# A banded-attention and SMeLU kernel on one core: wider bias matmuls, another layout for half of q, and a divided weight load one piece later

## The chip, the cores and the metric

The kernel runs on 1 core of one Trainium2 chip. The metric is the device time in microseconds (us) of one launch, as a median over several runs. Beside the times there is one profiled execution, from which all rows of the profile come.

The engines are called as the profile calls them: PE (matmuls), PEld (weight loads of the same engine), DVE (VectorE), ACT (ScalarE), POOL (GpSimd, which here issues nearly all loads) and SP (SyncE, which issues the stores and the transposing DMAs).

## The reference

```python
# q, k, v: (8, 8, 576, 64) float32; w_in: (512, 2048); w_out: (2048, 512)
scores = q @ k.T / sqrt(64), kept only where |query - key| <= 32, else -1e9
attn   = softmax(scores);  attn_out = attn @ v
x = attn_out.transpose(0, 2, 1, 3).reshape(4608, 512)
h = x @ w_in
g = h if h >= 1, 0 if h <= -1, else (h + 1)**2 / 4
out = g @ w_out                                # (4608, 512) float32
```

The first part is attention in a band of 65 keys around each query, the second a two-layer network over the 4608 rows of its output.

## The kernel before

**Attention.** Heads 0 to 3 live on partitions 0 to 63 and heads 4 to 7 on partitions 64 to 127; this is the index `h`, and `HD[0]`, `HD[1]` are the two partition ranges. q and k are brought to the form "head dimension on partitions" (`qT`, `kT`). For batch 0 PE does this: `tpose` transposes nine slices `j` of 64 (or 2 x 64) columns, and the result is copied out of PSUM by ACT or DVE (line 193). Where the source tile has nine slices of 128 columns, with both halves of heads side by side, `tpose` issues one 128-column transpose for each `j` (line 192); else two of 64 columns (line 190). The first half of batch 0's q (`q32`) is laid out for the former by `cast`, which changes it from float32 to bfloat16 on DVE and ACT. The second half of q and k (`qn[0, 1]`, `kn[0, 1]`, tiles `qh` and `kh`) is loaded by `load_half` as bfloat16 and is transposed in `tposes(0, (0, 1), (1, 1))` at step 1, by line 190.

`scores` computes blocks of 64 keys by 128 queries into two PSUM banks with matmuls of 64x64 tiles (line 230) and takes their exponential on ACT (line 238). Where its argument `eng` is None, the band is made beforehand: `add_mask` (line 209) writes a large negative bias into the same PSUM banks and the score matmuls are added to it. `eng` is None in all of batch 0, and for steps below 14; from then on DVE multiplies the exponentials by a mask (line 204). `add_mask` is called eight times: six times before step 4, and twice for the scores of batch 1 at the steps 12.5 and 13. `sums` multiplies by v and by ones (line 296), and its `end` divides through Ln and Exp on ACT (lines 302, 303) and a multiplication on DVE (line 308 or 311), which writes the rows of `xT`.

**The network.** The main loop counts steps `a`; eight steps make the first layer for 256 rows (`NF` = 8 pieces of 256 columns of w_in; line 490, wide steps line 515). Each step's result goes through ACT (line 534) and DVE (lines 540, 541; in five steps ACT's line 537 and DVE's 538) to `gT`. The second layer is interleaved (lines 450 and 465) and the attention of later batches is spread over the steps by the events `ev`. Step `a` needs w_in's columns 256a to 256a + 255 in the first eight steps. At a = 0 the pieces f = 0 and f = 1 are done together, first with the rows `y = 0` of `xT`, then with `y = 1`.

**The loads.** Every engine works in the order in which its instructions are written. POOL's order at the start is: k's first half, v of batch 0, then the list that `put` runs through:

```python
    cuts = [0, 256, 512, 768, 1024, 1280, 1536, DFF]
    w = [(load_w_in, c0, c1, h) for c0, c1 in zip(cuts, cuts[1:]) for h in range(2)]
    w[3] += ((0, 52, 64),)
    put(w[:4] + [(load_half, 1, t, h) for t in range(2) for h in range(2)] + w[4:])
```

So w_in comes in 14 loads, two for each range of columns, one for each half of the partitions; `w[0]` to `w[3]` are the columns of step 0, `w[4]` and `w[5]` (the third range of columns) those of step 2, and `w[12]` and `w[13]`, which are twice as wide, those of the steps 6 and 7. `w[3]` is issued as two DMAs, of 52 and of 12 partitions. Between `w[3]` and `w[4]` come four loads of the second halves of q and k. The program's loads from POOL go round eight semaphores, and an issue waits for the landing of the load eight places before it. After w_in come w_out's first pieces, and q and k of batch 1.

Of the kernel before, what the change touches and what calls it, by code (L numbers as in the profile page):

```python
# [8 lines left out]
BF = mybir.dt.bfloat16  # L9
# [5 lines left out]
def kernel(  # L15
# [19 lines left out]
    nc = tc.nc  # L35
    B, H, S, D = q.shape
# [11 lines left out]
    const = ctx.enter_context(tc.tile_pool(name="const", bufs=1))  # L48
# [10 lines left out]
    def two_banks(pool):  # L59
        return pool.tile([128, 2, 512], FP, name="bb", tag="bb")  # L60

    ident = const.tile([128, 128], BF, name="ident")
    ones = const.tile([128, 64], BF, name="ones")
    band = const.tile([128, 192], BF, name="band")
    bias = const.tile([128, 192], BF, name="bias")
    mask4 = const.tile([128, 8 * 128], BF, name="mask4")
# [8 lines left out]
    V, P, A = nc.vector, nc.gpsimd, nc.scalar  # L75


    qn, kn, vn = {}, {}, {}
    HD = (slice(0, 64), slice(64, 128))
# [40 lines left out]
    early = ctx.enter_context(tc.tile_pool(name="early", bufs=1))  # L120
# [24 lines left out]
    def put(todo):  # L145
        for fn, *x in todo:
            fn(*x)

    cuts = [0, 256, 512, 768, 1024, 1280, 1536, DFF]
    w = [(load_w_in, c0, c1, h) for c0, c1 in zip(cuts, cuts[1:]) for h in range(2)]  # L150
    w[3] += ((0, 52, 64),)
    put(w[:4] + [(load_half, 1, t, h) for t in range(2) for h in range(2)] + w[4:])
    put([(load_w_out, 0, k, k + 4) for k in (0, 4, 8)] + [(load_rows, 1, t) for t in range(2)] + [(load_w_out, 0, 12, 16)])
    put([(load_v, 1, n) for n in range(4)])
# [10 lines left out]
    def qkT(b, t):  # L165
        if t == 0:
            return qTs[b % 3][:, PAD:]
        if b not in kT:
            kT[b] = ktp.tile([128, NY * S], BF, name="kT")
        return kT[b]  # L170

    def tpose(b, n, t, copy, ps):


        half, part = divmod(n, 2)
        j0, j1 = ((0, 5), (5, 9))[part]
        if b:
            src = qn[b] if t == 0 else kn[b]
            src = [src[:, half + 2 * h] for h in range(2)]
            dst = qkT(b, t).rearrange("d (y e p j) -> d y e p j", y=2, e=2, j=9)[:, half, :, :, j0:j1]  # L180
            like = "d j (e p) -> d e p j"
        else:
            src = (qn, kn)[t][b, half]
            src = src if src.shape[1] == 9 else [src[:, h] for h in range(2)]
            dst = qkT(b, t).rearrange("d (y l p j) -> d l y p j", l=2, p=32, j=9)[:, half, :, :, j0:j1]
            like = "d j (p y) -> d y p j"
        for j in range(j0, j1):
            if isinstance(src, list):
                for h in range(2):
                    nc.tensor.transpose(ps[HD[h], j - j0], src[h][:, D * j:D * j + D], ident)  # L190
            else:
                nc.tensor.transpose(ps[:, j - j0], src[:, j], ident)
        return lambda: copy(dst, ps[:, :j1 - j0].rearrange(like, p=64 if b else 32))
# [10 lines left out]
            eng.tensor_mul(p, p, m)  # L204

    def add_mask(ps, n, w):
        for a in range(2):
            for h in range(2):
                nc.tensor.matmul(ps[h][HD[a], :n * w].rearrange("p (n j) -> p n j", n=n), ident[HD[h], HD[h]],  # L209
                                 bias[HD[h], 64 * h:64 * h + w].rearrange("p (n j) -> p n j", n=1)  # L210
                                 .to_broadcast([64, n, w]),
                                 start=True, stop=False, skip_group_check=True)

    def scores(b, ys, pars, cs, eng, pool=ps_s, w=128, ready=None):

# [98 lines left out]
    def flush():  # L314
        while muls:
            muls.pop(0)()
# [4 lines left out]
    def tp1(pool):  # L321
        if pool is ps_h:
            return pool.tile([128, 8, 128], BF, name="tp", tag="hp")
        return pool.tile([128, 2, 8, 128], BF, name="tp", tag="bb")[:, 0]
# [16 lines left out]
    def cast(x, nm, cut):  # L341

        y = early.tile([128, 9, 2, D], BF, name=nm)
        o, i = y.rearrange("p j h d -> p h j d"), x.rearrange("p h (j d) -> p h j d", d=D)
        V.tensor_copy(o[:, :, :cut], i[:, :, :cut])
        A.copy(o[:, :, cut:], i[:, :, cut:])
        return y.rearrange("p j h d -> p j (h d)")

    with tc.tile_pool(name="ps_p", bufs=1, space=bass.MemoryType.PSUM) as ps_p:
        keep_warm(11, ps_h, "hp")  # L350

        V.memset(qkT(0, 0).rearrange("d (y s) -> d y s", y=NY)[:, :, S // 2:352], 0.0)
        for b in range(LONG):
            V.memset(qkT(b, 0).rearrange("d (y s) -> d y s", y=NY)[:, :, S - PAD:], 0.0)
        V.memset(qkT(0, 1).rearrange("d (y s) -> d y s", y=NY)[:, :, S // 2:320], 0.0)
        qn[0, 0] = cast(q32, "qb", 5)
        qq = [tpose(0, n, 0, (A.copy, V.tensor_copy)[n], tp1(ps_h)) for n in range(2)]
        for x in qq:
            x()
        kk = [tpose(0, n, 1, (A.copy, V.tensor_copy)[n], tp1((ps_n, ps_p)[n])) for n in range(2)]  # L360
        keep_warm(1, ps_h, "hp")
        first = two_banks(ps_s)
        add_mask([first[:, h] for h in range(2)], 4, 128)
        for x in kk:
            x()
        scores(0, (0, 1), (0, 2), (0, 2), None, ready=first)
        scores(0, (0, 2), (0, 1), (2, 3), None, ps_n, 32)
        scores(0, (1, 2), (0, 2), (0, 2), None, ps_p)
        keep_warm(4, ps_h, "hp")
        e0 = sums(0, 0, 0, TB)  # L370
        e1 = sums(0, 1, 0, TB, ps_p)
        keep_warm(5, ps_h, "hp")
        e0()
        e1()
# [44 lines left out]
    for b in range(LONG + 1, B):  # L419
        a = sl[5 * (b - 1) - 7] - 17  # L420
# [75 lines left out]
    for a in range(NF * NB + 2 * NF):  # L496
        wide = WIDE[0] <= a < WIDE[1]
        eng = None if a < 14 else V
        post = [] if a >= 40 else [x for n, x in pairs if n == a] + [a - NF] * (a >= 2 * NF + 2)
        for b, x in loads.get(a, []):  # L500
            if x < 2:
                load_nat(b, x)
            else:
                for n in range(4):
                    load_v(b, n)
        if a == 0 or a > 3:
            flush()
        if a < NF * NB:
            if wide:
                n, f = divmod(a - WIDE[0], 2 * NF)  # L510
                t = WIDE[0] // NF + 2 * n
                r0 = TB * t % RING
                hp = ps_h.tile([128, 2, TB], FP, name="hp", tag="hp")
                for n, kk in enumerate((0, 2, 1, 3)):
                    nc.tensor.matmul(hp.rearrange("p n t -> p (n t)"), w_in[:, kk, 128 * f:128 * f + 128],  # L515
                                     xT[:, kk, r0:r0 + 2 * TB], start=n == 0, stop=n == 3)
                g = gT[:, f, home(t):home(t + 1) + 1:home(t + 1) - home(t)]
            else:
                t, f = divmod(a, NF)
                r0 = TB * t % RING  # L520
                if a in (0,):
                    hps = [ps_h.tile([128, 2, TB], FP, name="hp", tag="hp") for _ in range(2)]
                    for y in range(2):
                        for n in range(2):
                            project(hps[n], f + n, r0, [(j, y + 2 * m) for j in range(2) for m in range(2)], y == 0, y == 1)
                elif not hps:
                    pool, tag = (ps_o, "op") if a == 6 else (ps_h, "hp")
                    hps = [pool.tile([128, 2, TB], FP, name="hp", tag=tag)]
                    project(hps[0], f, r0, [(j, kk) for j in range(2) for kk in (0, 2, 1, 3)], True, True)
                hp = hps.pop(0)  # L530
                g = gT[:, 2 * f:2 * f + 2, home(t)]

            rr = ewp.tile([128, 2, TB], FP, name="rr")
            A.activation(rr, hp, AF.Relu, scale=0.5, bias=0.5)  # L534
            mx = ewp.tile([128, 2, TB], FP, name="mx")
            if a in two_on_act:
                A.activation(mx, rr, AF.Square)
                V.scalar_tensor_tensor(g, hp, 1.0, mx, op0=ALU.max, op1=ALU.min)
            else:
                V.tensor_max(mx, hp, rr)  # L540
                V.scalar_tensor_tensor(g, rr, 1.0, mx, op0=ALU.min, op1=ALU.mult)  # L541
        flush()
        run(a)
        for x in post:
            if x < 16:
                pair(x)
            else:
                for j in range(4):
                    unit(4 * x + j)
        if a >= 40:  # L550
            n = 3 if a < 72 else 4
            for x in range(done, done + n):
                unit(x)
            done += n
        run(a + 0.5)
        for x in xps.get(a, []):
            xpose(*x)
# [30 lines left out]
```

## Time and profile before

| | |
|---|---|
| median of 8 runs | 307.54 us (306.85 to 308.46) |
| the profiled execution's own time | 307.93 us |
| its span | 306.2 us |
| PE busy | 292.6 us (96%) |
| DVE, ACT, POOL busy | 241.4, 190.6, 77.6 us |
| granted PE clock | 1.00 in the five windows read, 0 to 306.2 us |

The span is the time from the first to the last instruction in the profile; 1.73 us of the profiled execution lie around it, and the execution itself lies 0.39 us above the median. Places in the span are given in us from its start.

PE's busy time in five windows of the span is 10.11 of 12.00 us (0 to 12), 11.17 of 14.30 us (12 to 26.3), 15.70 of 15.70 us (26.3 to 42), 242.98 of 248.00 us (42 to 290) and 12.68 of 16.20 us (290 to 306.2).

### The profile page before, as it was taken

Reading aid. Unit: us, or ns where it says so; the run is one execution under the profiler, and the core shown is the slowest. Engines: PE = TensorE matmul, PEld = TensorE weight load, DVE = VectorE, ACT = ScalarE, POOL = GpSimd, SP = SyncE. Lnnn points to the kernel's source line nnn. Section 1 sums busy time; section 2 is a strip of 40 time slices with the busy share of each in tenths; the row PEclk is TensorE's granted clock in tenths of the full one; section 3 lists DMA queues with packets and bytes.
Section 4 is the critical chain, followed back from the end, with each engine's and each line's share of the span. In section 5 each row is a group of like instructions: output and inputs, shape, how many; then the busy total and the mean of one; then the engine's idle time right before and its main releaser. Section 6 shows DMA issues by size and latency. Waiting matters only on the chain.

```text
span 306.2 us, 7809 instructions
## 1 busy us (share of the span) xinstructions
PE 292.6 (96%) x3286; PEld 174.8 (57%) x3324; DVE 241.4 (79%) x378; ACT 190.6 (62%) x318; POOL 77.6 (25%) x93
## 2 busy tenths in 40 slices
PE   8788999999999999999999999999999999999995
PEld 3467878877666766544445444444445444446644
DVE  4278868888888999999988888888888888788700
ACT  3687786738856778667766766665667654444311
POOL 8795771019008206403700730000000000000000
PEclk9999999999999999999999999999999999999999
DMA  9999999999999999995999997551011010010121
GB/s 149 182 177 200 187 182 172 173 166 139 136 202 90 172 149 148 161 157 108 166 125 166 116 171 77 113 112 36 34 36 37 34 36 35 34 36 34 58 82 69
DMA packets 137251, 35.67 MB, mean 117 GB/s; under 512 B 122240, under 2 KB 132992, under 8 KB 137216
## 3 DMA queue, kind: packets, MB, share of 16 engines
q0 software_dynamic: 103056, 18.06, 80.0%
q1 hardware_dynamic: 34016, 16.81, 26.4%
q8 instruction: 26, 0.43, 0.6%
q10 hardware_dynamic: 144, 0.29, 0.4%
q14 instruction: 9, 0.07, 0.1%
HBM read 36.70 MB, written 9.44 MB: 151 GB/s over the span
## 4 chain that ended last, share of the span: by engine, by line
PE 89%; DMA 4%; POOL 3%; issue 2%; ACT 0%; POOLq 0%; ACTq 0%
PE op L450 34%; PE hp L515 23%; PE hp L490 17%; PE bb L296 6%; PE op L465 5%; DMA w_in<-in_moe_w_in_dram 4%; PE bb L230 2%; POOL w_in L112 2%; PE op L441 1%; POOL vn L107 1%; PE tp L190 1%; POOL kh L86 0%; PE bb L209 0%; PE bb L255 0%; POOL step L134 0%
## 5 line engine op out<-in xcount | busy, mean ns | idle before, releaser
L534 ACT ACTIVATE rr<-hp 128x512 f32<-128x512 f32 x144 | 85.6, 595 | 85.6 <-PE hp L515 49.5
L450 PE MATMUL op<-w_out,gT 128*128 128x512 bf16 x460 | 119.5, 379 | 5.0 <-issue 4.8
L540 DVE TENSOR_TENSOR mx<-hp,rr 128x512 f32<-128x512 f32 x139 | 95.7, 689 | 28.1 <-ACT rr L534 26.5
L541 DVE SCALAR_TENSOR_TENSOR gT<-rr,mx 128x512 bf16<-128x512 f32 x139 | 96.4, 694 | 4.8
L515 PE MATMUL hp<-xT,w_in 128*128 128x512 bf16 x320 | 82.1, 379 | 0.0
L450 PEld LDWEIGHTS <-gT 128*128 128x128 bf16 x496 | 46.1, 98 | 47.6
L490 PE MATMUL hp<-xT,w_in 128*128 128x256 bf16 x512 | 66.2, 273 | 2.9 <-DMA w_in<-in_moe_w_in_dram 2.4
L490 PEld LDWEIGHTS <-w_in 128*128 128x128 bf16 x512 | 49.2, 98 | 18.3 <-DMA w_in<-in_moe_w_in_dram 2.0
L515 PEld LDWEIGHTS <-w_in 128*128 128x128 bf16 x320 | 31.3, 98 | 37.8
L99 POOL DMA_DIRECT2D qn<-in_q_dram x12 | 14.6, 1221 | 91.9 <-DMA kT<-kn 89.7
L238 ACT ACTIVATE pt<-bb 128x1024 bf16<-128x1024 f32 (+1 forms) x33 | 32.9, 1002 | 5.0 <-PE bb L230 3.6
L107 POOL DMA_DIRECT2D vn<-in_v_dram x32 | 27.5, 888 | 5.6 <-DMA w_out<-in_moe_w_out_dram 3.1
L308 DVE TENSOR_TENSOR xT<-bb,rc 128x512 bf16<-128x512 f32 (+1 forms) x32 | 21.0, 657 | 9.5 <-ACT rc L303 8.6
L454 ACT COPY osb<-op 128x512 f32<-128x512 f32 x31 | 18.0, 581 | 12.2 <-PE op L450 11.8
L303 ACT ACTIVATE rc<-lr 128x512 f32<-128x512 f32 (+2 forms) x40 | 23.5, 587 | 1.3
L302 ACT ACTIVATE lr<-bb 128x512 f32<-128x512 f32 (+2 forms) x40 | 22.0, 550 | 0.4 <-PE bb L296 0.3
L204 DVE TENSOR_TENSOR pt<-pt,mask 128x1024 bf16<-128x1024 bf16 (+1 forms) x33 | 20.3, 614 | 0.5 <-ACT pt L238 0.5
L296 PE MATMUL bb<-pt,ones 64*64 64x256 bf16 (+3 forms) x352 | 19.4, 255 | 0.1
L296 PE MATMUL bb<-pt,vn 64*64 64x128 bf16 (+3 forms) x712 | 18.3, 204 | 0.1
L296 PEld LDWEIGHTS <-ones 64*64 64x64 bf16 x352 | 10.2, 105 | 12.5 <-issue 12.5
L296 PEld LDWEIGHTS <-vn 64*64 64x64 bf16 x712 | 16.7, 107 | 0.3 <-DMA vn<-in_v_dram 0.3
L465 PE MATMUL op<-w_out,gT 128*128 128x256 bf16 x128 | 16.3, 273 | 0.0
(61 smaller groups left out, 137.8 us busy)
## 6 DMA issues: line engine op xcount, KB each, us to landing
out_dram<-osb SPq DMA_DIRECT2D x35, 256.0 KB, 2.4
vn<-in_v_dram POOLq DMA_DIRECT2D x32, 144.0 KB, 11.1
qn<-in_q_dram POOLq DMA_DIRECT2D x12, 288.0 KB, 7.1
kn<-in_k_dram POOLq DMA_DIRECT2D x12, 288.0 KB, 9.0
w_in<-in_moe_w_in_dram POOLq DMA_DIRECT2D x11, 128.0 KB, 5.0
w_out<-in_moe_w_out_dram POOLq DMA_DIRECT2D x4, 256.0 KB, 8.9
w_out<-in_moe_w_out_dram POOLq DMA_DIRECT2D x2, 512.0 KB, 12.3
kh<-in_k_dram POOLq DMA_DIRECT2D x4, 144.0 KB, 4.9
```

Of the source, the lines that this page charges most:

```text
L107: nc.gpsimd.dma_start(out=vn[b][64 * a:64 * a + 64, :, h], in_=v[b, y:y + 2].rearrange("y s d -> (y s) d") .rearrange("(c r) d -> r c d", ...
L238: A.activation(p, ps[:, :, :w * n].rearrange(like, y=m), AF.Exp, scale=D ** -0.5)
L296: nc.tensor.matmul(bb[HD[h], a, o + c0:o + c1], ones[HD[a]] if c is None else vn[b][HD[a], c, h], p(a, h), start=n == 0, stop=True, skip_g ...
L302: A.activation(lr[:, :, :D0], bb[:, :, D0:2 * D0], AF.Ln)
L303: A.activation(rc[:, :, :D0], lr[:, :, :D0], AF.Exp, scale=-1.0)
L450: nc.tensor.matmul(op[tt], gT[:, j, home(tt // 2), 128 * (tt % 2):128 * (tt % 2) + 128], w_out[:, j], start=j == 0, stop=j == 15)
L465: nc.tensor.matmul(o[:, tt], gT[:, j, p, 128 * tt:128 * tt + 128], w_out[:, j, 256 * half:256 * half + 256], start=not done, stop=len(done ...
L490: nc.tensor.matmul(hp[:, j], w_in[:, kk, 256 * f + 128 * j:256 * f + 128 * j + 128], xT[:, kk, r0:r0 + TB], start=first and n == 0, stop=l ...
L515: nc.tensor.matmul(hp.rearrange("p n t -> p (n t)"), w_in[:, kk, 128 * f:128 * f + 128], xT[:, kk, r0:r0 + 2 * TB], start=n == 0, stop=n == 3)
L534: A.activation(rr, hp, AF.Relu, scale=0.5, bias=0.5)
L540: V.tensor_max(mx, hp, rr)
L541: V.scalar_tensor_tensor(g, rr, 1.0, mx, op0=ALU.min, op1=ALU.mult)
```

## The change

It has three parts. `add_mask` uses a new constant `fold`, two 64x64 identities side by side, so that one matmul with a 64x128 tile writes both partition halves of a bank: two matmuls for each call where there were four. `fold` is written by two DVE additions after `cast`. At step 0 DVE copies the second half of q (`qn[0, 1]`) into a new tile `y`, with both halves of heads side by side for each `j`, so that `tpose` takes line 192's way for it: nine transposes of 128 columns in place of eighteen of 64. And the load that is divided into 52 and 12 partitions is `w[4]` in place of `w[3]`.

```diff
+    fold = const.tile([128, 128], BF, name="fold")
...
-    w[3] += ((0, 52, 64),)
+    w[4] += ((0, 52, 64),)
...
     def add_mask(ps, n, w):
-        for a in range(2):
-            for h in range(2):
-                nc.tensor.matmul(ps[h][HD[a], :n * w].rearrange("p (n j) -> p n j", n=n), ident[HD[h], HD[h]],
-                                 bias[HD[h], 64 * h:64 * h + w].rearrange("p (n j) -> p n j", n=1)
-                                 .to_broadcast([64, n, w]),
-                                 start=True, stop=False, skip_group_check=True)
+        for h in range(2):
+            nc.tensor.matmul(ps[h][:, :n * w].rearrange("p (n j) -> p n j", n=n), fold[HD[h]],
+                             bias[HD[h], 64 * h:64 * h + w].rearrange("p (n j) -> p n j", n=1)
+                             .to_broadcast([64, n, w]),
+                             start=True, stop=False, skip_group_check=True)
...
         qn[0, 0] = cast(q32, "qb", 5)
+        for h in range(2):
+            V.tensor_add(fold[:, HD[h]], ident[:, HD[0]], ident[:, HD[1]])
         qq = [tpose(0, n, 0, (A.copy, V.tensor_copy)[n], tp1(ps_h)) for n in range(2)]
...
         if a == 0 or a > 3:
             flush()
+        if a == 0:
+            y = early.tile([128, 9, 2, D], BF, name="qr")
+            for h in range(2):
+                V.tensor_copy(y[:, :, h], qn[0, 1][:, h].rearrange("p (j d) -> p j d", d=D))
+            qn[0, 1] = y.rearrange("p j h d -> p j (h d)")
         if a < NF * NB:
```

## The prediction

> **What bounds the kernel now.** I read the page's chain first (the chain of work that ended last, shares by engine), then the same chain in order of time for the start, which all three parts of the change touch.
>
> ```profile
> PE 89%; DMA 4%; POOL 3%; issue 2%; ACT 0%; POOLq 0%; ACTq 0%
> ```
>
> ```profile
> 8.17 6.10 DMA w_in<-in_moe_w_in_dram
> 14.27 0.28 issue
> 14.55 4.21 POOL w_in L112 x7
> 18.77 7.48 DMA w_in<-in_moe_w_in_dram
> 26.25 0.05 issue
> 26.29 1.92 PE hp L490 x16
> ```
>
> The columns are start and length in us. Up to 26.25 the chain consists of loads: the issue at 8.17 is the 52-partition part of w[3]; it lands at 14.27, 0.28 later POOL may issue w[6] (eight places on, the same semaphore), seven more issues follow, and the last, w[13], lands at 26.25. From 26.29 on it is PE: in the windows 26.3 to 42 PE is busy for 15.70 of 15.70 us. So the run is a loading stage with its end at w[13], and 279.9 us of PE work in a fixed order behind it. An edit moves the end only if it moves w[13]'s landing or changes PE's time after 26.29.
>
> The waits in the window 26.3 to 45 show what is spare before w[13]:
>
> ```profile
> PE hp L490 <- DMA w_in<-in_moe_w_in_dram: 1.0, 1, 1.0
> ```
>
> PE stood idle for 1.0 us there, with everything earlier done. DVE is busy without a break from 24.12 to 30.3 and then has 1.17 us of idle time, ACT has 1.36 at 30.87. Anything before 26.29 that becomes later by less than 1 us is swallowed.
>
> **Mask matmuls.** Eight calls of four become eight of two. Six are issued before 26.29, under the cover just named (without it each would cost what follows). Two, at 39.43 and 40.97, are on the path. The timeline there:
>
> ```profile
> 39.43 0.11 PEld L209 LDWEIGHTS <-ident 64*64 64x64 bf16 x4 [0.21 <-issue]
> 39.43 0.41 PE L209 MATMUL bb<-bias,ident 64*64 64x512 bf16 x4
> 39.46 0.44 PEld L230 LDWEIGHTS <-kT 64*64 64x64 bf16 x16
> 39.67 0.39 PE L230 MATMUL bb<-qT,kT 64*64 64x128 bf16 x16
> ```
>
> All four mask matmuls begin at 39.43 to 39.44, one on each quarter of the array, and the scores begin 0.24 us later. So the two that are taken away cost nothing today: the path holds one stream of 512 columns, and the two 64x128 matmuls still have it. What is added is a change of tile shape between mask and scores, which now share 64x64. Its price is seen elsewhere, after a 512-column matmul that begins at 7.40:
>
> ```profile
> 7.39 0.10 PEld L339 LDWEIGHTS <-warm 128*128 128x128 bf16 x1
> 7.72 0.11 PEld L209 LDWEIGHTS <-ident 64*64 64x64 bf16 x4 [0.23 <-issue]
> ```
>
> The next shape's weights load 0.32 us after the matmul's start, not right behind its own weights, as line 230's do at 39.46. With the second mask matmul at 39.44 the scores begin at 39.44 + 0.32 = 39.76 instead of 39.67: +0.09 for a call. Lower end: no gap between these two shapes, 0 (not below, since the 512 columns stay). Upper end: the two halves don't run side by side, the second begins at 39.67, the scores at 39.99, +0.32. I take +0.09, since 64-row tiles do run side by side in the row above: two calls, **+0.18**, ends 0 and +0.64.
>
> The rule that speaks against the change is in the Trainium skill, "TensorEngine Tiling (Array Packing)", Tiling Modes, Key Properties: a change of tiling mode, not just of tile, drains TensorE. The 0.21 us before 39.43 agree with it for 128x128 to 64x64. The page gives no time; by it alone the term is a loss of unknown size, and without it the term would be 0.
>
> `fold` costs DVE two additions of 128x64. The nearest row is line 141's 128x128 addition, 0.23 us, so at most 0.46 for both, between 5.87 (end of the cast) and 6.76, where DVE idles 0.89 us for the transposes. Without that cover the first qT copy would be 0.46 later, still inside the 1.0 us.
>
> **Nine transposes.** Line 190's eighteen for q's half and the eighteen for k behind it:
>
> ```profile
> 15.97 0.69 PE L190 MATMUL tp<-ident,qh 128*64 128x128 bf16 x18
> 16.50 0.98 PE L190 MATMUL tp<-ident,kh 128*64 128x128 bf16 x18
> ```
>
> Eighteen take 0.69 us, with 0.22 for a single one, so nine pairs are 0.056 us apart: the two 64-column ones run side by side. Nine of 128 columns (line 192, 0.80 us at 5.92) need as long. Nothing is saved; k's stay as they are and wait for their load (the gap inside the second row). A change of shape now falls between q's and k's transposes, 0.10 us (line 192 to 190 at 6.65), inside that wait.
>
> The copies are new work for DVE, 128x576 bfloat16 each. Bounds: line 204's 0.614 us for 128x1024 gives 0.35, the cast's 0.69 for 128x640 gives 0.62. They wait for qh, which lands at 9.68 + 4.9 = 14.6 and 10.38 + 5.0 = 15.4. Behind them on DVE stands step 0's maximum:
>
> ```profile
> 16.27 0.69 DVE L540 TENSOR_TENSOR mx<-hp,rr 128x512 f32<-128x512 f32 x1 [1.75 <-ACT rr L534]
> ```
>
> The second copy ends at 15.75 to 16.0, before 16.27: hidden in 1.75 us of idle time. PE's transposes, at 15.97 today, wait up to 0.1 for it. Were qh to land 1 us later, line 540 and the transposes would be up to 0.8 late; cover: PE's 1.0. So **0**.
>
> **The divided load.** The number of DMAs stays, and from w[5] on each stands at its old place in the queue and the semaphores. Moved ahead by one place are both qh, both kh and w[4]'s first part; the issue of w[6] now waits for the whole of w[3]. POOL's rows and the landing times (from the tile view of those windows):
>
> ```profile
> 8.17 0.74 POOL L112 DMA_DIRECT2D w_in<-in_moe_w_in_dram  x1
> DMA to landing us min/median/max: 6.1/6.1/6.1
> 8.85 0.61 POOL L112 DMA_DIRECT2D w_in<-in_moe_w_in_dram  x1
> DMA to landing us min/median/max: 5.6/5.6/5.6
> 14.55 0.61 POOL L112 DMA_DIRECT2D w_in<-in_moe_w_in_dram  x1 [0.99 <-DMA w_in<-in_moe_w_in_dram]
> DMA to landing us min/median/max: 4.7/4.7/4.7
> ```
>
> The parts land at 14.27 and 14.44; the piece before (7.57 + 5.1) at 12.7. Neighbouring whole pieces land 0.7 apart (w[4] 12.32 + 5.1, w[5] 12.95 + 5.2). So w[3] whole lands at 13.4 at the earliest, at 14.27 + 0.7 = 15.0 at the latest, and at 14.4 if the same bytes end at the same place, which I take. w[6] is then issued at 13.65, 15.25 or 14.7, against 14.55. What that does to w[13] is bounded by w[6]'s own row: it lands at 19.25, 1.1 behind w[5], where neighbours are 0.7 apart; at most 0.4 of that is the queue running dry. An earlier issue gains at most 0.4, a later one costs at most its 0.7; the middle one costs 0.15 if nothing is queued and 0 if enough is. I take **+0.1**, ends -0.4 and +0.7.
>
> The page "DMA: Bandwidth & Descriptors", section "Why a DMA increments its semaphore by 16 and not by 1", says that a DMA is spread over the largest number of engines up to 16 that divides its slowest dimension: 13 engines for 52 partitions, 12 for 12. No row here shows engines singly. By it, dividing costs the busiest engines one row in five wherever it stands, and by w[5] the sum is the same.
>
> **Sum.** 307.93 (the profiled execution) + 0.18 + 0 + 0.1 = 308.2; that execution lies 0.39 above the median, so the median goes from 307.54 to **307.8**.
>
> **Rivals.**
> - *A late DMA engine at the last piece (slower).* The divided load landed 1.0 us late (6.1 against 5.1), and in the DMA view of 12 to 13.4 there is this:
>
> ```profile
> q8 instruction: 1, 0.02, 4.3%
> ```
>
> One fetch of instructions goes through the same engines; there are 26 packets of that queue for 6,610 PE instructions, 254 each. The next falls in 21.2 to 21.6, and w[11], issued at 17.56, lands after 5.8. The change removes 24 mask instructions and 18 transposing ones (weight loads counted) before 26; at some 450 in the 14.3 us of the second window, 42 are 1.3 us. The second fetch moves towards w[12] and w[13], with less time to catch up. Price: up to the 1.0 that the first one cost, with the masks +1.2, 308.7. It decides once w[13] lands after 27.0. Against it: w[13] carries the second fetch already, and the queue behind it is full.
> - *Mask halves one after the other (slower, by little).* +0.64 + 0.1: 308.3. Against it: the quarters that run together at 39.43.
> - *w[3] free of that fetch (faster).* If the fetch falls after w[3], that lands at 13.4, w[6] is issued 0.9 earlier and w[13] lands 0.4 earlier; if the late engine recovers the whole 1.0, it is -0.8: 306.7 to 307.3 with the masks.
> - *The masks do take time off PE.* All that could be taken off the path is the two 0.24 us before the scores, -0.5; the 512 columns speak against it. I count it with the one before.
>
> **How the numbers follow.** A measurement of this kernel can tell about 0.3%, 0.9 us, from no change, so "same" is 306.6 to 308.5. Forecast 0.50, within that. Late engine 0.22, of which 0.20 is slower. Mask halves in turn 0.10, of which 0.03 is slower, with a late w[3]. Earlier loads 0.18, of which 0.09 is faster. The forecast's own upper ends (0.64 and 0.7 together) add 0.01 slower. Faster 0.09, same 0.67, slower 0.24. The range, from 307.54 - 0.4 = 307.1 to 307.54 + 0.64 + 0.6 = 308.8, holds the forecast, the halves in turn, most of the late engine and half of the earlier loads.
>
> **What would show it.** Right: w[13]'s landing and the first line 490 matmul after it at 26.0 to 26.7; scores 0.3 us behind the masks at about 39.5 and 41, where they are 0.24 now; nine line 192 transposes of some 0.7 us near 16; DVE's line 540 of step 0 near 16.3; PE filled as before from there. Wrong: PE waiting for w_in beyond 27, a new wait in PE's order after 26.29 (for w_out or batch 1's q and k, which land close to their use), or scores 0.5 us behind the masks.

## The result, and the profile after

| | before | after |
|---|---|---|
| median | 307.61 us (306.48 to 308.89, 32 runs) | 310.11 us (308.56 to 311.49, 11 runs) |
| ratio | | 1.0085, 95% interval 1.0066 to 1.0104 |
| profiled execution: own time, span | 307.93, 306.2 us | 309.46, 307.5 us |
| start of step 6's matmuls | 26.29 us | 27.32 us |
| from there to the end of the span | 279.9 us | 280.2 us |
| around the span | 1.8 us | 2.0 us |

The change makes the kernel 2.5 us slower, outside the predicted range. The profiled execution is one of the shorter ones after the change; it accounts for 1.5 us: 1.0 in the loading stage, 0.3 behind it, 0.2 outside the span.

The page's chain of work that ended last, after, has the same engines as before:

```profile
PE 88%; DMA 5%; POOL 3%; issue 2%; ACT 0%; POOLq 0%; ACTq 0%
```

In order of time (start, length in us) its first part has another link:

```profile
8.76 6.47 DMA qh<-in_q_dram
15.23 0.28 issue
15.51 3.61 POOL w_in L113 x6
19.12 8.15 DMA w_in<-in_moe_w_in_dram
27.27 0.05 issue
27.32 1.92 PE hp L492 x16
```

Before, the first link was w[3]'s part, then w[6]'s issue. Now it is q's half: it lands at 15.23, and POOL's issue of w[7] had waited for it. w[13] is issued 0.35 us later and lands 1.0 later. One late DMA engine is not the reason for the rest: by the landing records, which have one entry for each of the 16 engines, fifteen had done their part of w[13] by 26.98, and by 25.39 before. From 21 to 24 us the engines together moved 127 GB/s, where they had moved 165 before; why, no run here shows. The waits after (who waited for whom: total us, times, longest), window 14 to 28, show that and a second thing that was not there before:

```profile
PE hp L492 <- DMA w_in<-in_moe_w_in_dram: 1.3, 3, 0.6
...
POOL w_in L113 <- DMA qh<-in_q_dram: 1.1, 1, 1.1
...
PE bb L296 <- issue: 0.8, 1, 0.8
```

PE waits 0.6 us for w[13], where it waited 1.0: part of that time has gone into the last line. Its "issue" means that PE waited for nothing that the profile shows, in the middle of `sums`, whose operands were there. The second fetch of instructions begins at 23.52 (21.36 before) and its packet takes until 25.23; PE goes on at 26.51. It had run out of instructions (the evidence stands below, under the number of PE instructions). In this execution that did not set the start of step 6, as w[13] landed only at 27.27. The changed kernel has 50 PE instructions fewer in all (32 in the masks, 18 in the transposes).

The masks, by PE's timeline:

```profile
40.54 0.39 PE L209 MATMUL bb<-bias,fold 64*128 64x512 bf16 x2
40.86 0.42 PE L230 MATMUL bb<-qT,kT 64*64 64x128 bf16 x16
41.21 0.28 PE L492 MATMUL hp<-xT,w_in 128*128 128x256 bf16 x1
```

Both matmuls begin at 40.54, so the halves run side by side, and the scores follow 0.32 behind, as predicted; from mask to next step it is 0.67 instead of 0.57 (39.43 to 40.00 before).

### The profile page after: what moved, and what is told of

It reads as the page before. It is cut to its first block, busy times and chain, and to the rows that moved or that the text cites. A ratio compares the mean times of both kernels' runs of the same rounds, so it can differ in the third digit from the quotient of the medians.

```text
span 307.5 us, 7763 instructions
## 1 busy us (share of the span) xinstructions
PE 293.5 (95%) x3261; PEld 174.8 (57%) x3299; DVE 242.4 (79%) x382; ACT 190.9 (62%) x318; POOL 77.6 (25%) x93
## 4 chain that ended last, share of the span: by engine, by line
PE 88%; DMA 5%; POOL 3%; issue 2%; ACT 0%; POOLq 0%; ACTq 0%
PE op L452 34%; PE hp L522 22%; PE hp L492 17%; PE bb L296 6%; PE op L467 5%; DMA w_in<-in_moe_w_in_dram 3%; PE bb L230 2%; DMA qh<-in_q_dram 2%; POOL w_in L113 2%; PE op L443 1%; POOL vn L108 1%; PE tp L191 1%; POOL kh L87 0%; PE bb L209 0%; PE bb L255 0%
```

## The experiments

Every kernel ran beside the kernel before on the same chip, in five rounds; ratios are to that. What came out first is the place of the divided load, which costs by itself. PE's supply of instructions also changes; the profiles show the wait, but what it costs is less well shown. Idle time from either can also close PE's clock.

### Each part alone

`mask_only` is the change without the hunks for `qr` and for `w[4]`:

> The kernel before with the wide mask matmuls alone (32 PE instructions fewer in all, 12 of them before 12.3 us, 24 before 26). Theory A, the count of PE instructions sets when the next instructions are fetched, and a fetch late in the load of w_in delays its last piece: first two fetches later than 12.3 and 21.4 us, last w_in piece lands at 26.6 to 27.3, median +0.6 to +2 us over before. Theory B, the place of the division is the cause: +0.2 us, which is two mask calls on the path at 0.1 each. Theory C, the changes of tile shape themselves cost more than the profile shows: +1 to +2.5 us with w_in landing at 26.2 as before.

Ratio 1.0045 (1.0021 to 1.0070), 308.69 us. Second fetch at 23.45; PE waits 0.87 us for instructions, until 25.87; w[13] lands at 25.47. So the loads were early, and the late fetch set the start of step 6 (26.13). That start is no later than before (26.29), and the profiled execution, at 308.06, is one of the shorter of the twelve: where the others lose their time the profile does not show.

`q_only` is the hunk for `qr` alone:

> The kernel before with q's copies and nine transposes alone (18 PE instructions fewer, all after 15 us). Theory A: first fetch at 12.3 as before, the second later than 21.4 by up to 1 us, median 0 to +1 us. Theory B: 0. A further rival, the copies on DVE delay step 0: line 540's successor at 16.5 or later and +0.3 us or more.

Ratio 1.0046 (1.0021 to 1.0070), 308.75 us. Second fetch at 23.79, and on PE:

```profile
26.01 0.22 PE L296 MATMUL bb<-pt,ones 64*64 64x64 bf16 x3 [1.28 <-issue]
```

The copies themselves are hidden (see below), and w[13] had landed at 25.88. This profiled execution, too, is as long as the one before (307.94 against 307.93). Of theory A the late second fetch is right in both kernels, and more than its price for q. The rest is not: in `mask_only` the first fetch came at 11.93, not after 12.3, and w[13] landed early instead of at 26.6 or later. Of the twelve executions of `q_only` four, and of `mask_only` two, have a lower mean clock (0.994 or less, see below); the others have medians of 308.0 and 308.6, against 307.58 for the kernel before beside them.

`div_only` is `w[3]` to `w[4]` alone:

> The kernel before with the divided load moved to the third piece alone (no PE instruction changes). Theory A: fetches at 12.3 and 21.4 us as before, last w_in piece within 0.3 of 26.25, median within 0.5 us of before. Theory B: POOL's issue of the eighth w_in DMA waits for q's half, the last w_in piece lands at 26.6 or later, and most of the 2.5 us are here.

Ratio 1.0054 (1.0028 to 1.0079), 309.19 us. Fetches at 12.86 and 20.97, so not a matter of instructions; w[13] issued at 19.55 and landed at 27.85. Theory A alone falls, and B is right that most of the loss lies in the division, but not in its wait. The chain:

```profile
8.38 6.50 DMA w_in<-in_moe_w_in_dram
14.88 0.28 issue
15.16 2.45 POOL w_in L112 x4
17.61 0.14 issue
17.75 1.80 POOL w_in L112 x3
19.55 8.30 DMA w_in<-in_moe_w_in_dram
```

Here it is w[3], whole, that lands late, at 14.88, and w[6] that waits for it, not w[7] for q's half. w[6] is issued at 15.16 (14.55 before), w[13] 0.78 us later than before, and it lands 1.6 later; from 21 to 24 us the engines moved 112 GB/s. This execution also shows the effect on PE's clock. In windows of the timeline (length, then busy us of PE, PEld, DVE, ACT, POOL, the granted clock, DMA share, GB/s):

```profile
24.00:27.60 3.60, 1.65 (x52) 1.15 (x44) 3.02 (x6) 3.27 (x7) 1.54 (x3) 1.00 1.29 186
27.60:31.00 3.40, 3.10 (x15) 2.24 (x16) 1.77 (x4) 0.88 (x2) 1.77 (x3) 0.50 1.38 202
31.00:34.50 3.50, 3.50 (x34) 3.09 (x33) 1.53 (x3) 1.74 (x3) 2.87 (x5) 1.00 1.22 208
```

PE was busy for 1.65 of 3.60 us, then its clock was granted at half for 3.41 us (the trace's clock record), with 15 matmuls in 3.40 us where the next window has 34 in 3.50. From step 6 to the end of the span it is 281.4 us here and 279.9 before.

### Giving each cause back

`after_padded` fills PE's instructions up to their number before:

```diff
         for h in range(2):
+            nc.tensor.matmul(ps[h][:, :1], fold[HD[h]], bias[HD[h], 64 * h:64 * h + 1], start=True, stop=False, ...)
+        for h in range(2):
             nc.tensor.matmul(ps[h][:, :n * w]...
...
+                for _ in range(2 if half else 1):
                     nc.tensor.transpose(ps[:, j - j0], src[:, j], ident)
```

> The changed kernel with as many PE instructions as before at each place: each mask call has two more matmuls of one column, and each of the nine transposes is done twice. Theory A: fetches back at 12.3 and 21.4 us, last w_in piece at 26.0 to 26.6, median 307.6 to 308.2, which is 2 us under the changed kernel. Theory B and C: no better than the changed kernel, 309.5 to 311.

Ratio 1.0046 (1.0025 to 1.0067), 308.88 us. Second fetch at 20.21, no wait for instructions; but w[13] still lands at 27.28, behind POOL's 1.1 us of waiting for q's half. By the ratios about half of the loss is taken back, with intervals that touch (1.0066 and 1.0067). In the profiles step 6 begins at 27.33, as after the change (27.32), so they do not show where that half was.

`after_w3` is the changed kernel with the division back at `w[3]`, `padded_w3` is `after_padded` with it:

> The changed kernel with the division back at w_in's fourth load, nothing filled up. Theory A2: last w_in piece at 25.4 to 26.3 and PE out of instructions for about 1 us until 25.9 to 26.5, some executions with a half-clock stretch; median 308.5 to 309.2, which is 1 to 1.5 us under the changed kernel. Rival, the division's place has nothing to do with it once the count has changed: 309.7 to 310.5.

> The changed kernel with its PE instructions filled up to the count before (as in after_padded) and the division put back at w_in's fourth load. Theory A2 (two causes: the count of PE instructions decides whether PE runs out of instructions near 25 us; the place of the division decides how late the last w_in piece is issued and lands): last w_in piece at 25.4 to 26.3, no wait of PE for instructions near 25 us, median 307.7 to 308.1, of which 0.2 are the two mask calls. Rival, the wide masks or the copies on DVE cost by themselves: 308.5 or more.

`after_w3`: 1.0004 (0.9979 to 1.0029), 308.37 us; w[13] lands at 25.58, but the second fetch came at 25.25 and PE waited 2.15 us for it, until 27.55. That profiled execution is the longest of its twelve (309.79); over all of them the kernel is 0.04% slower than the one before, at most 0.29%, and the median lies under the 308.5 to 309.2 that I expected. `padded_w3`: **0.9986 (0.9965 to 1.0007), 307.59 us**, 307.27 to 308.23; fetch at 20.98, w[13] lands at 24.76, step 6 begins at 25.36. With the division back and the instructions filled up the wide masks and the new layout cost nothing that can be measured. As a table of ratios:

| | instructions missing | filled up |
|---|---|---|
| division at w[4] | 1.0085, again 1.0087 | 1.0046 |
| division at w[3] | 1.0004 | 0.9986 |

The second value of the first cell is `after_again`, the changed kernel once more:

> The changed kernel again: 309.5 to 310.5, with the second fetch at 23 us or later, PE out of instructions near 25 to 26.5, and the last w_in piece landing at 26.8 or later.

310.42 us (1.0054 to 1.0121). Second fetch at 23.85, PE out of instructions until 26.16 (1.04 us), w[13] issued at 19.17 behind q's half (15.11), landed at 26.68, 0.1 short of what I expected. Both delays are there again.

### What the division does

```diff
 no_division:  (the line for w[3] left out)
 div_w4_even:  w[4] += ((0, 32, 64),)   in place of w[3]'s
 div_last:     w[13] += ((0, 52, 64),)  in place of w[3]'s
 slot_w4:      no division; behind w[4] one load more, of w_out's first 16 rows by 128 columns, into a spare tile
```

> The kernel before with no w_in load divided. Theory A2, the division at the fourth load keeps one of its loads off the engine that carries the first fetch: without it the wait for that engine is as in div_only, last w_in piece at 27 or later, median 308.8 to 309.5. Rival, it is the small extra load in the third piece that hurts: as before, 307.6.

> The kernel before with the third piece's first load divided 32 and 32 instead of w[3] 52 and 12. Ring theory: a division there uses up one of eight places, so that POOL's w[6] and w[7] wait for w[3] and q's half, which the first fetch delays; even parts do the same: w[13] issued at 19.1 to 19.6, landing at 26.3 to 27.9, median 309.0 to 309.4, as div_only. Rival, the uneven parts load the DMA engines unevenly: with even parts as without division, 307.5 to 307.8.

> The kernel before with w[13], the last w_in load, divided 52 and 12 instead of w[3]. Ring theory: no issue of w_in waits earlier than without division, so as no_division: w[13]'s first part issued at 18.2 to 18.8, median 307.5 to 307.9. Rival, a 52 and 12 division costs wherever it delays what PE waits for: 308.5 or more.

> The kernel before with no division and, behind w[4], one extra load of 16 partitions by 128 columns into a spare tile. Ring theory: the extra load takes the place that the division took, so 308.8 to 309.4 with w[6] and w[7] waiting as in div_only. Rival, it is what the division does to w_in's own descriptors: 307.5 to 307.9.

| kernel | ratio, interval | median us | w[13] issued, landed |
|---|---|---|---|
| no_division | 0.9995, 0.9970 to 1.0020 | 307.52 | 18.66, 25.19 |
| div_w4_even | 1.0046, 1.0014 to 1.0079 | 309.68 | 19.45, 28.32 |
| div_last | 0.9993, 0.9967 to 1.0018 | 307.60 | 18.80 (first part), 26.03 (second) |
| slot_w4 | 1.0041, 1.0015 to 1.0067 | 309.00 | 18.83, 25.95 |

My idea that the division at w[3] protects something was wrong: without any it is as before. Nor is it uneven parts (even ones cost the same) or what dividing does to w_in's transfer (dividing w[13] costs nothing, one foreign load of 4 KB costs the same). What is left is the place in the round of eight semaphores: all kernels with an extra load at w[4] are slower than the kernel before, whatever that load is. A load more behind w[4] makes each later issue wait for a load that stands one place later: w[7] for q's first half instead of w[3], w[8] for its second, and so on. These are the loads that the first fetch of instructions holds up. In the profile after it begins at 13.21 and its packet takes 0.97 us; the landing records of that q half show fifteen DMA engines done by 14.21 and the last at 15.23. (The same count would come from dividing w[3]; there the extra place stands ahead of q's half, and w[7] waits for the second part of w[3].)

The profile of `slot_w4` does not show this way, though. Its w[6] waited for w[3] (14.10) and was issued at 14.38, and w[13] landed at 25.95, both a little earlier than before. What makes its span 1.1 us longer is another wait, near 120 us, for a transposing load of a later batch, which is not in the profile before (in `padded_q` it takes 0.7):

```profile
PE bb L234 <- DMA kT<-kn: 1.1, 1, 1.1
```

So that an extra load costs at this place is measured by the ratios; the way from the late issue to the time is shown in the profiles of the changed kernel, `after_padded`, `div_only` and `div_w4_even`, and open for `slot_w4`.

### What the number of PE instructions does

`padded_q` is `q_only` with each of the nine transposes issued twice. `mask_fill` is `mask_only` with the first edit below, `before_fill` the kernel before with it, `fill_no_division` that without the division, `before_fewer` the kernel before with the second edit:

```diff
+        for _ in range(12):
+            nc.tensor.matmul(z[:, :16], warm[:, :128], warm[:, :16], start=True, stop=True)
...
-        keep_warm(4, ps_h, "hp")
+        keep_warm(1, ps_h, "hp")
...
-        keep_warm(5, ps_h, "hp")
+        keep_warm(2, ps_h, "hp")
```

> The kernel before with q's copies and nine transposes, each issued twice so that PE has as many instructions as before; masks and division as before. If the missing PE instructions are all that q_only paid for: no wait of PE for instructions near 25 us and 307.2 to 307.7, which is 1 us or more under q_only. If the copies on DVE cost by themselves: 308.5 or more.

> The kernel before with the wide masks and twelve spare matmuls of 16 columns just ahead of step 0, which give back 24 PE instructions. If the count alone decides: second fetch at 20 to 22.5, no wait for instructions near 25 us, median 307.6 to 308.1, of which 0.2 are the two mask calls on the path. If the wide masks cost by themselves: 308.5 to 309.

> The kernel before with six of its spare matmuls (those that keep PE busy at 9 to 13 us) left out: 12 PE instructions fewer ahead of the first fetch, nothing else changed. If the count alone decides: second fetch at 23 us or later, PE without instructions for about 1 us near 25 to 26.5, median 308.3 to 309. If the count must go with the new masks or layout: second fetch at 21 to 22, 307.5 to 308.

> The kernel before with twelve spare matmuls of 16 columns just ahead of step 0 (24 PE instructions more), nothing else changed. If the filling is what makes the last w_in piece land at 24.7: second fetch at 20 to 21, last piece at 24.5 to 25.3, step 6 from 25.2 on, median 306.7 to 307.1, under the kernel before. If it was the masks or chance: 307.3 to 307.9.

> The same filling without the divided load: as before_fill within 0.3 us, if the division at the fourth load does nothing, as no_division said; 0.5 us or more above it if the division helps once the fetch is early.

| kernel | ratio, interval | median us | second fetch | PE out of instructions until | w[13] landed |
|---|---|---|---|---|---|
| q_only | 1.0046, 1.0021 to 1.0070 | 308.75 | 23.79 | 26.01 | 25.88 |
| padded_q | 0.9991, 0.9966 to 1.0016 | 307.80 | 20.91 | - | 26.37 |
| mask_only | 1.0045, 1.0021 to 1.0070 | 308.69 | 23.45 | 25.87 | 25.47 |
| mask_fill | 0.9989, 0.9973 to 1.0006 | 307.17 | 20.10 | - | 24.74 |
| before_fewer | 1.0006, 0.9989 to 1.0024 | 307.50 | 23.72 | 25.94 | 26.56 |
| before_fill | 1.0003, 0.9986 to 1.0021 | 307.67 | 20.15 | - | 25.40 |
| fill_no_division | 0.9993, 0.9977 to 1.0010 | 307.05 | 22.20 | 24.63 | 25.22 |

Filling takes back the whole loss of the masks and of q's layout; the two pairs of intervals do not overlap, and `padded_w3` has both without a loss. So neither the change of tile shape nor the copies are the cause.

That PE ran out of instructions is seen from the place of the wait. In all seven profiles that have it, PE stops after the same number of instructions in the trace, 703 (705 in `after_again` and `before_fewer`), whatever the kernel had issued, and goes on 1.3 to 1.5 us after the second fetch's packet has ended.

What this wait costs is another matter. `before_fewer` missed my expectation of the time: with twelve instructions fewer the fetch is late and PE stands still, and nothing is lost. In its profile w[13] landed after PE had gone on:

```profile
25.94 0.23 PE L296 MATMUL bb<-pt,vn 64*64 64x96 bf16 x2 [1.01 <-issue]
...
26.61 0.61 PE L490 MATMUL hp<-xT,w_in 128*128 128x256 bf16 x4 [0.27 <-DMA w_in<-in_moe_w_in_dram]
```

By the order of the work a late fetch can cost only where its wait ends after w[13]'s landing, or where its idle time closes PE's clock; that is argued, not measured. In both profiles of the changed kernel the wait ended before w[13] landed (26.51 and 26.16 against 27.27 and 26.68). The loss itself rests on the ratios of `mask_only` and `q_only`, which ran on one chip; `after_w3`, `before_fewer` and `fill_no_division`, which run out too and lose nothing, ran on others, and so did the filled kernels `padded_q` and `mask_fill`. That this loss depends on the chip is not excluded. Nor does the number act in one direction: `fill_no_division` has more instructions than before and runs out too, early enough to lose nothing. What starts a fetch stays open; counted in the trace, PE had executed 497 to 614 instructions when the second one began in the profiles where it did not run out, and 632 to 703 in the seven where it did. And `before_fill` missed the 306.7 to 307.1 that I hoped for; `fill_no_division` lies 0.6 us under it, which neither side of my expectation had. The medians of `div_w4_even`, `padded_q`, `mask_fill`, `after_w3` and `div_warm` lie outside my ranges by up to 0.4 us, none of them nearer to the rival's. No kernel here is shown to beat the one before.

### PE's clock

`div_warm` puts spare matmuls into the two waits of `div_only`:

```diff
         if a == 0 or a > 3:
             flush()
+        if a in (5, 6):
+            keep_warm(a - 1, ps_o, "op")
```

> The kernel with the division moved alone (div_only), with four and five spare 512-column matmuls in PE's waits ahead of the steps 5 and 6. If the half-clock stretch of 3.4 us after those waits is the cause of the slow part of the executions: no execution with a mean clock of 0.994 or less, the times above 310 us are gone, median 308.8 to 309.3. If the idle time isn't what closes the clock gate: a quarter of the executions still at 310.5 to 311.

No execution of 12 has a mean clock of 0.994 or less (2 of 8 in `div_only`, 5 of 12 in `div_w4_even`, 2 of 12 in `slot_w4`, 1 of 11 in `after_padded`: at 10 in 43, none of 12 would come about by chance about once in 24), and the longest is 310.37 us; but the median is 309.37, ratio 1.0045 (1.0020 to 1.0071): the matmuls take the longest executions away and leave most of the delay. (The profiled execution, its shortest, has w[13] issued at 19.12 and landed at 26.30.) In the changed kernel 7 of 20 executions have such a mean clock, with 311.4 us in the middle, where the other 13 have 308.2 to 311.3; of 147 executions of the kernel before, 4 do. That mean is what a single 3.4 us stretch at half clock gives in 307.

The Trainium skill, "TensorE: Matmul & The Clock Gate", Part 1, describes a gate that looks at free-running windows of 3.413 us, which agrees with the length of the stretch; its rule of thumb in the same part is to have no idle gaps of more than about 3.4 us. That rule would not have warned of this case: PE's longest single waits at the stretch in `div_only` were 1.1 and 1.2 us, the second reaching 0.3 us into it.

The traces show more. In all 19 profiles the granted clock changes on a grid of 3.41 us, counted from each trace's first clock record. In the step of this grid just ahead of a half-clock stretch PE was busy for 0.42 (`div_only`), 0.45 (`after_padded`) and 0.46 (`div_w4_even`) of the step; in every other step up to 301 us, over 1,600 in all, for 0.52 or more. So in these traces the busy share of one step tells the two cases apart, and it depends on where the grid happens to lie: the 2.15 us of `after_w3` fall into two steps with 0.55 and 0.82, and its clock stays full.

## Why the prediction was wrong

**The step that failed is the divided load's.** I wrote that "from w[5] on each stands at its old place in the queue and the semaphores", and priced the one wait of w[6], at +0.1 (-0.4 to +0.7). The place is the old one, but what stands eight places before w[7] to w[11] is one load later: in both profiles of the change w[7] waits for q's first half, which the first fetch delays (15.23 and 15.11). And the cap of 0.7 at w[13] was wrong even for the wait that I did price: in `div_only` w[6] was issued at 15.16, inside my 13.65 to 15.25, and w[13] landed 1.6 us later than before. I had at most 0.4 us for the queue running dry; from 21 to 24 us alone the engines moved 159 kB less than before (112 against 165 GB/s), by an estimate 0.8 us at the 189 GB/s of the microsecond ahead of it, and the cause of that stays open. In time, `div_only` measured 0.54% of 307.6, 1.7 us (0.9 to 2.4), against my +0.1. `slot_w4`, in which only a place is taken, has 0.41% (0.15 to 0.67), though its profile has another wait.

**The cover was counted for work, not for supply.** "Anything before 26.29 that becomes later by less than 1 us is swallowed" was right for what PE, DVE and ACT were given: the copies took 0.81 us in all, and step 0's maximum even began earlier than before:

```profile
15.25 0.81 DVE L513 COPY qr<-qh 128x576 bf16<-128x576 bf16 x2 [0.58 <-DMA qh<-in_q_dram]
15.98 0.69 DVE L547 TENSOR_TENSOR mx<-hp,rr 128x512 f32<-128x512 f32 x1
```

It left out two things: PE's instructions themselves may be late, by 0.8 to 2.2 us of idle time in seven profiles, and idle time that is "swallowed" by a wait can still close the clock behind it, 1.5 us in `div_only`'s profile. How much of the 2.5 us is due to them is not shown; filling up the instructions took back about 0.4%.

**The rival of the late DMA engine** had the fetch move towards w[12] and w[13], priced at 1.2 and deciding once w[13] lands after 27.0. The fetch did move (21.36 to 23.52), w[13] landed at 27.27 in one profile of the change and 26.68 in the other. But the fetch's own lateness is not what made w[13] late: it is late in `div_only` with the second fetch at 20.97, and after the change the last engine is only 0.3 us behind the fifteenth (27.27 and 26.98), where it was 0.9 behind before. The moved fetch starved PE instead, a wait that I had not thought of. So this rival, to which I gave 0.22, had the direction right, and the fetch's move, but not the way to w[13].

**What held:** the masks, +0.18 predicted, with the time behind step 6 at 280.1 to 280.2 us in `after`, `after_again`, `mask_only`, `after_w3` and `padded_w3` against 279.9 before; halves side by side; nine transposes as long as eighteen (0.68 us at 16.12 against 0.69); `fold` and the copies hidden.

**Not settled:** why the DMA engines are slower at 21 to 24 us; 0.2 us outside the span, which the kernels with both the wide masks and the copies have (2.0 us around it) and those with one of them have not (1.8); and where the executions of `mask_only` and `q_only` that were not profiled lose their time.

## What to carry to other kernels

Before moving, dividing or adding a load, write down for each later issue which landing it waits for, eight places back or however many the program has: an extra place anywhere shifts all waits behind it, and one of them may be a load that is late. Taking instructions away from PE moves its fetches; look where they fall, and treat an "issue" wait in the middle of ready work as a sign that it may have run dry. If several kernels stop after the same number of instructions, it did. When idle time is called cover, ask whether PE is still busy enough to keep its clock. And look at what the profiled execution lost before calling its waits the cause of a difference between medians.

## What the runs showed of the hardware that I had not expected

- PE's instructions come through the same DMA engines as the data, 16 KB for about 254 of them; a fetch holds one engine up by about 1 us (landing records: fifteen engines by 14.21, one at 15.23), and PE ran dry for 0.8 to 2.2 us in seven profiles, each time after 703 to 705 instructions.
- A 3.41 us step of the clock's grid in which PE was busy for 0.42 to 0.46 of it was followed by 3.41 us at half clock, one with 0.52 or more never; in `div_only` no single wait was longer than 1.2 us. The same kernel shows it in some executions and not in others.
- A change of tile shape costs the scores 0.08 us behind a 512-column matmul (0.32 against 0.24), twice in this kernel's path after the first loads.
